# A recurrence with decay and a squared-ReLU network in one kernel: eight fewer matmuls on zeros ahead of the first dense layer, and new engine orders up to unit 4

## The chip, the core and the metric

The kernel runs on one core of a Trainium2 chip. Its engines work side by side: TensorE (PE) multiplies matrices, with weight loads (PEld) that overlap its matmuls; VectorE (DVE), ScalarE (ACT) and GpSimd (POOL) work element by element; SyncE (SP) and POOL issue transfers (DMA) between the chip's memory and the core's SBUF. PE writes into PSUM, in banks, from which DVE and ACT read.

The metric is the device time of one execution in microseconds (us). Each kernel is run several times, and the median counts. A profile is one further execution, recorded by the hardware profiler.

## The reference

```python
B, H, S, D = 4, 8, 768, 48
state = np.zeros((B, H, D, D)); y = np.zeros_like(q)
for t in range(S):
    state = alpha[:, :, t, :, None] * state + np.einsum('bhd,bhe->bhde', k[:, :, t], v[:, :, t])
    y[:, :, t] = np.einsum('bhd,bhde->bhe', q[:, :, t], state)
x = y.transpose(0, 2, 1, 3).reshape(B * S, H * D)     # 3072 x 384
r = np.maximum(x @ w_in, 0.0)                         # 384 -> 2048
out = (r * r) @ w_out                                 # 2048 -> 384
```

A linear attention with a decay `alpha` per channel, then two dense layers with a squared ReLU between them. `alpha` lies between 0.8 and 1.

## The kernel before

**Units.** Time is cut into three stretches of 256 steps. A *unit* is one stretch of one of the four sequences, so there are twelve, numbered 0 to 11 (units 0 to 3 are the first stretch of the four). Each unit passes through the same stages, and the work of several units overlaps.

**Names.** Every operation has a name, `kind` plus unit (and part), and these names make up the tables of the change. In a unit g:

- `lda ldk ldq ldv`: the four loads (384 KB each). Units 1 and 2 load from POOL's list, all others from SP's.
- `pr` (product of two neighbours' alpha), `ln` (its logarithm), `m1i`, `m1s` (matmuls that sum logarithms along time, into PSUM bank W), `ei ea ec es` (exponentials of the sums), `lm lb` (a difference that replaces `m1s` from unit 4 on), `bk aq` (one more factor alpha): the *decays*. Units 0 and 1 do without pairs: one matmul step `m1` (for unit 0 two, `m10`, `m11`, by halves of the heads).
- `ekm eqm`: keys and queries times their decays. `tr`: their transposes, on PE for units 0 to 2 (with copies `et` out of PSUM), from unit 3 on as two transposing DMAs `tr0 tr1` that SP issues. `vc`: v cast to bf16.
- `p0` (unit 0: also `p1`): the scores, keys against queries, into banks X and Z; `mk0 mk1`: causal mask on the two halves, out of PSUM.
- `kv`: the new state's matmuls (into Z from unit 1 on; from unit 3 on they are part of the `y` of the unit before); `sa sc sd`: sums and decay of the state.
- `y`: the attention's output into X; `xe`: out of PSUM; `xt`, `xv`: its transpose (units 0 to 3 on PE with a copy `xv`, then by DMA).
- `s1_g_u`, u = 0 to 7: the first dense layer, six matmuls of 256 columns into one of two banks H in turn; `re`: ReLU out of the bank; `sq`: the square, mostly of two groups at once.
- `s2_g_j_s`: the second layer, four matmuls of 384 columns; four groups make one output half j in the single bank O; `oe`: out of PSUM; `out`: the store.
- `win0 win1 wout0 wout1`: halves of the two weights, loaded and cast to bf16 from POOL's list. `s2` groups 0 and 1 read the first half of `wout`, 2 and 3 the second.
- `~512`, `~256` on PE: a matmul of that many columns on zeros into bank O. It waits for nothing but the zeros themselves, and nothing reads what it writes.

**What sets the order.** `TABLES` (L203 to L262) holds one list per engine, written out by name. `Program.schedule` takes each engine's queue from it word by word; an operation that several engines can do (`pr`, `sd`, `re`, `sq`, `oe`, `xv`, `et`, `vc`, `bk`) runs on the engine whose list names it. Dependencies come from the tiles that an operation reads and writes; `place` turns them into waits on semaphores ahead of the operation. An engine works through its list in order, so an operation that waits holds up all that stand behind it. That holds for SP and POOL too: a transfer is issued when all ahead of it in the list have been issued or done.

The fillers are placed here:

```python
if word[0] == "~":
    after, n = filler[0], int(word[1:])
    o = Op({"pe": (filler[1](n), 0)}, 0, "fill")
```

Some loads are gated by the landing of another:

```python
AFTER = {1: (0, "a"), ("win", 0): (0, "k"), ("win", 1): (0, "k"), 2: ("win", 0), ("wout", 0): ("win", 1),
         ("wout", 1): (2, "k"), 3: ("wout", 0)}
```

So `wout1` waits for unit 2's keys, and unit 3's loads for `wout0`. A bank is reused only after what was in it has been read: `s1_g_u` waits for the `re` of the group two before it in its bank, `s2_g_j_0` for the `oe` of the half before it, `m1s` for the exponentials that read `m1i`'s sums.

Of the kernel before, what the change touches and what calls it, by code (L numbers as in the profile page):

```python
# [24 lines left out]
class Program:  # L25
# [144 lines left out]
    def emit(self):  # L170
# [44 lines left out]
        s1_5_7 s1_5_6 s2_5_0_0 s2_5_0_1 s2_5_0_2 s1_6_0 s1_6_1 p0_7 s1_6_2 s1_6_3 s2_5_0_3 s1_6_4 s1_6_5 y7 m1i9
        s2_5_1_0 s2_5_1_1 s2_5_1_2 s2_5_1_3 s1_6_6 p0_8 s1_6_7 s2_6_0_0 s2_6_0_1 s1_7_0 s2_6_0_2 s1_7_1 s2_6_0_3
        s1_7_2 s1_7_3 y8 s1_7_5 s1_7_4 s2_6_1_0 s2_6_1_1 m1i10 s2_6_1_2 s1_7_7 s1_7_6 s2_6_1_3 s1_8_1 s1_8_0
        s2_7_0_0 s2_7_0_1 s2_7_0_2 s2_7_0_3 m1i11 s1_8_3 s1_8_2 p0_9 s2_7_1_0 s2_7_1_1 s1_8_4 s2_7_1_2 y9 s1_8_5
        s2_7_1_3 s1_8_6 s1_8_7 s2_8_0_0 s2_8_0_1 p0_10 s2_8_0_2 s1_9_1 s1_9_0 s2_8_0_3 s1_9_3 s1_9_2 y10 s1_9_5
# [872 lines left out]
```

## Time and profile before

| | us |
|---|---|
| median of 3 runs | 177.73 (177.08 to 179.05) |
| the profiled execution | 174.4 |
| its span, first to last instruction | 172.7 |
| first matmul of the first dense layer | 17.59 |
| last piece of the chain of waits | 170.39 |

Start times in the views below count from the span's start. The profiled execution is 1.7 us longer than its span, and 3.3 us shorter than the median of the runs. The granted TensorE clock in the page is 9 tenths or more in every slice. The share of the sixteen DMA engines in use is nine tenths or more in nearly every slice up to 100 us. In a row of the timeline the columns are start, length, engine, line, operation, output and inputs with their shapes, the number of instructions merged, and in brackets the idle time of the engine before it with what ended it. Line numbers are those of the kernel: `s1` is L965, `s2` L1005, ReLU L973 (ACT) and L975 (DVE), squares L983 and L987, scores L838, masks L849, fillers L1061, `pr` L565 and L567, `sd` L815, loads L456, weights L432, transposing DMAs L652.

### The profile page before, as it was taken

Reading aid. Unit: us, or ns where it says so; the run is one execution under the profiler, and the core shown is the slowest. Engines: PE = TensorE matmul, PEld = TensorE weight load, DVE = VectorE, ACT = ScalarE, POOL = GpSimd, SP = SyncE. Lnnn points to the kernel's source line nnn. Section 1 sums busy time; section 2 is a strip of 40 time slices with the busy share of each in tenths; the row PEclk is TensorE's granted clock in tenths of the full one; section 3 lists DMA queues with packets and bytes.
Section 4 is the critical chain, followed back from the end, with each engine's and each line's share of the span. In section 5 each row is a group of like instructions: output and inputs, shape, how many; then the busy total and the mean of one; then the engine's idle time right before and its main releaser. Section 6 shows DMA issues by size and latency. Waiting matters only on the chain.

```text
span 172.7 us, 5090 instructions
## 1 busy us (share of the span) xinstructions
PE 167.6 (97%) x2232; PEld 130.4 (76%) x2234; DVE 122.3 (71%) x202; ACT 113.7 (66%) x201; POOL 26.9 (16%) x37
## 2 busy tenths in 40 slices
...
GB/s 145 351 292 212 270 233 172 283 286 297 204 213 191 232 257 168 273 243 188 255 165 128 285 149 245 270 90 286 277 66 238 174 77 181 4 53 87 0 93 91
DMA packets 71030, 33.36 MB, mean 193 GB/s; under 512 B 67552, under 2 KB 67808, under 8 KB 71008
## 3 DMA queue, kind: packets, MB, share of 16 engines
...
## 4 chain that ended last, share of the span: by engine, by line
PE 79%; DMA 16%; POOL 3%; issue 1%; DVE 0%
PE psO L1005 34%; PE psWH L965 33%; DMA wout<-in_moe_w_out_dram 5%; DMA win<-in_moe_w_in_dram 5%; DMA raw<-in_k_dram 3%; POOL raw L456 3%; PE psX L735 2%; PE psZ L703 2%; DMA raw<-in_alpha_dram 2%; PE psX L838 2%; PE psX L724 2%; PE psX L935 2%; PE psZ L838 1%; PE psWH L574 1%; PE psX L909 0%
## 5 line engine op out<-in xcount | busy, mean ns | idle before, releaser
L965 PE MATMUL psWH<-xt,win 128*128 128x256 bf16 x576 | 73.0, 274 | 0.0
L1005 PE MATMUL psO<-wout,gt 128*128 128x384 bf16 x368 | 68.2, 326 | 0.6 <-DMA wout<-in_moe_w_out_dram 0.6
L965 PEld LDWEIGHTS psWH<-xt,win 128*128 128x128 bf16 x576 | 65.2, 145 | 4.6 <-ACT xt L923 0.4
L973 ACT ACTIVATE rr<-psWH 128x512 bf16<-128x512 f32 x70 | 41.3, 595 | 21.9 <-PE psWH L965 20.8
L1005 PEld LDWEIGHTS psO<-wout,gt 128*128 128x128 bf16 x368 | 35.0, 98 | 19.0 <-DMA wout<-in_moe_w_out_dram 0.8
L987 ACT ACTIVATE gt<-rr 128x1024 bf16<-128x1024 bf16 (+1 forms) x31 | 26.9, 890 | 3.5 <-DVE rr L975 3.1
L975 DVE TENSOR_SCALAR rr<-psWH 128x512 bf16<-128x512 f32 x26 | 17.7, 688 | 10.0 <-PE psWH L965 9.7
L983 DVE TENSOR_TENSOR gt<-rr 128x1024 bf16<-128x1024 bf16 (+1 forms) x29 | 17.2, 597 | 9.6 <-ACT rr L973 9.4
L631 POOL CAST vbf<-raw 128x768 bf16<-128x768 f32 x9 | 8.1, 899 | 68.3 <-DMA raw<-in_v_dram 68.3
L849 DVE TENSOR_TENSOR pm<-psX,caus 128x1024 bf16<-128x1024 f32 x12 | 14.6, 1220 | 4.0 <-PE psZ L838 4.0
L849 DVE TENSOR_TENSOR pm<-psZ,caus 128x1024 bf16<-128x1024 f32 x12 | 14.6, 1219 | 3.4 <-PE psZ L838 3.4
L1012 ACT ACTIVATE osb<-psO 128x384 f32<-128x384 f32 x14 | 6.9, 491 | 10.1 <-PE psO L1005 8.8
L1061 PE MATMUL psO<-zero 128*128 128x512 bf16 (+1 forms) x32 | 9.9, 437 | 1.5 <-DVE zero L376 1.3
L894 ACT ACTIVATE xbf<-psX 128x768 bf16<-128x768 f32 x10 | 8.1, 808 | 4.5 <-PE psX L724 4.1
L636 DVE TENSOR_TENSOR qks<-raw,eq 128x384 bf16<-128x384 f32 x18 | 10.5, 587 | 0.4 <-ACT eq L611 0.3
L641 DVE TENSOR_TENSOR qks<-raw,ek 128x768 bf16<-128x768 f32 x11 | 10.5, 954 | 0.1
L585 ACT ACTIVATE ek<-psWH 128x384 f32<-128x384 f32 x10 | 4.9, 489 | 5.9 <-PE psWH L574 3.8
L567 POOL TENSOR_TENSOR prd<-raw 128x384 f32<-128x384 f32 x6 | 6.2, 1035 | 16.3 <-DMA raw<-in_alpha_dram 16.3
L1014 DVE COPY osb<-psO 128x384 f32<-128x384 f32 x9 | 5.0, 555 | 4.8 <-PE psO L1005 4.6
L594 DVE TENSOR_TENSOR ek<-ek,raw 128x384 f32<-128x384 f32 x9 | 5.0, 553 | 3.7 <-ACT ek L585 3.7
L568 ACT ACTIVATE lab<-prd 128x384 bf16<-128x384 f32 x10 | 5.2, 518 | 2.4 <-POOL prd L567 1.4
L1061 PEld LDWEIGHTS psO<-zero 128*128 128x128 bf16 x34 | 3.2, 109 | 4.5 <-issue 1.9
...
## 6 DMA issues: line engine op xcount, KB each, us to landing
...
```

Of the source, the lines that this page charges most:

```text
L631: add("pool", lambda e: e.tensor_copy(vout, vin), 830, p0 + 900, reads=[("raw", r, 3)], writes=[("vbf", vb)], name=f"vc{g}", alts={"act": ...
L636: add("dve", lambda e, j=j, dst=dst: e.tensor_tensor(dst, RAW[r][:, 2, :, j, :].rearrange("p (n x) d -> p n x d", x=2), EQ[la][:, j].rearr ...
L641: add("dve", lambda e, a=a, E=E: e.tensor_tensor(QKS[qs][:, a, :, :, 0:D], RAW[r][:, 1 + a].rearrange("p h j d -> p j h d"), E[la][:].rear ...
L849: add("dve", lambda e, hf=hf, psT=psT: e.tensor_tensor(PM[pm][:, hf].rearrange("p r n j t -> p (r n) (j t)"), psT[:, :, :].rearrange("p r ...
L894: add("act", lambda e: e.activation(XBF[x2][:], psX[:, :, 0:HD], AF.Copy), act_ns(2 * HD), p0 + 6100, reads=[("ps", "X", 0), ("ps", "X", 1 ...
L965: ins = pe.matmul(psH[hb][:, i * T:(i + 1) * T], WIN[:, kk, hidden(fj)], mov, start=(kk == 0), stop=(kk == KT - 1))
L973: add("act", lambda e, hb=hb, rr=rr: e.activation(rr, psH[hb], AF.Relu), act_ns(512), pu + 600, reads=[("ps", "H", hb)], writes=[("rr", rb ...
L975: alts={"dve": (lambda e, hb=hb, rr=rr: e.tensor_scalar(rr, psH[hb], 0.0, None, ALU.max), dve_ns(512))})
L983: add("dve", lambda e, dst=dst, sq=sq: e.tensor_tensor(dst, sq, sq, ALU.mult), 148 + k * 267, pu + 1200, reads=[("rr", rb, h) for h in ran ...
L987: "act": (lambda e, dst=dst, sq=sq: e.activation(dst, sq, AF.Square), act_ns(k * 512))})
L1005: ins = pe.matmul(psS, GT[gt][:, fj, j, :], WOUT[:, fj, :], start=(fj == 0), stop=(fj == FT - 1))
L1061: pr.schedule(TABLES, (zero, lambda n: lambda pe: pe.matmul(psO[:, 0:n], ZERO[:, 0:128], ZERO[:, 0:n], skip_group_check=True)))
```

## The change

Only the five lists of `TABLES` are changed; no operation and no dependency is, apart from the fillers.

- On PE, the fillers ahead of unit 0's first layer go from thirty of 512 and four of 256 columns to twenty-six of 512.
- On PE, up to unit 4, `m1`, `s1` and `s2` groups change places: `m1i2` stands behind `s1_0_6` and `xt1`, `m1s2` behind `s1_1_0`; `s1_1_4` stands where `s1_1_5` stood, and `s1_1_5` and `s1_1_6` now stand ahead of `s2_0_0_2`; `p0_3` and `p0_4` stand one group earlier.
- Between engines: `pr2` from POOL to DVE, `sd1` from DVE to POOL ahead of `wout1` and `ldv2`; `pr4` and `pr6` from DVE to POOL, `pr7` from POOL to DVE; `vc6` from POOL to ACT; `re`, `sq`, `oe` and `xv` of units 0 to 4 are dealt anew between ACT and DVE (among them `sq0_1`, `re0_6` and `oe1_0` to DVE; `re0_4`, `sq0_3`, `oe0_1` and `xv3` to ACT).
- On DVE, `eqm0_4` stands behind `mk1_3`, `mk0_3`, `re2_5` and `sq2_1`.
- On SP, `lda5` stands ahead of `ldq4` and `ldk4`, `ldv4` behind unit 3's two transposes, `ldk5` and `out0_1` ahead of `lda6`.

Lines of a list that only break elsewhere are left out:

```diff
--- before
+++ after
 TABLES = {
     "pe": """
-        ~512 ~512 ~512 ~512 ~512 ~512 ~512 ~512 ~512 m10_0 m11_0 ~512 ~512 ~512 tr00_0 ~512 ~512 ~512 tr10_0 ~512
-        ~512 ~512 ~512 tr11_0 p0_0 ~256 ~256 kv0 tr01_0 ~512 ~512 ~512 ~512 ~512 p1_0 m11 ~256 y0 ~512 ~512 ~512
-        ~512 ~512 tr0_1 xt0 tr1_1 ~512 ~256 s1_0_0 s1_0_1 p0_1 s1_0_2 s1_0_3 kv1 s1_0_4 s1_0_5 y1 m1i2 s1_0_6 xt1
-        s1_0_7 m1s2 s1_1_0 s1_1_1 tr0_2 s1_1_2 s1_1_3 tr1_2 s2_0_0_0 s1_1_5 s2_0_0_1 p0_2 s2_0_0_2 s2_0_0_3 s1_1_7
-        s1_1_4 kv2 s2_0_1_0 m1i3 s2_0_1_1 s2_0_1_2 s2_0_1_3 s1_1_6 m1s3 y2 s2_1_0_0 m1i4 s2_1_0_1 xt2 s2_1_0_2
-        s2_1_0_3 s1_2_1 s1_2_0 s2_1_1_0 s1_2_3 s1_2_2 m1i5 s2_1_1_1 s1_2_4 p0_3 s1_2_5 s1_2_6 s2_1_1_2 s2_1_1_3 y3
-        s1_2_7 s2_2_0_0 xt3 m1i6 s2_2_0_1 s1_3_1 s1_3_0 s2_2_0_2 s1_3_3 s1_3_2 s2_2_0_3 p0_4 s1_3_5 s1_3_4 s2_2_1_0
-        s2_2_1_1 s2_2_1_2 s2_2_1_3 y4 s1_3_7 s1_3_6 s2_3_0_0 s2_3_0_1 p0_5 m1i7 s2_3_0_2 s2_3_0_3 s1_4_1 s1_4_0 y5
-        s1_4_3 s1_4_2 s2_3_1_0 s2_3_1_1 s1_4_4 s1_4_5 s2_3_1_2 s2_3_1_3 s1_4_6 s1_4_7 s2_4_0_0 s1_5_0 s1_5_1
...
+        ~512 ~512 ~512 ~512 ~512 ~512 ~512 ~512 ~512 m10_0 m11_0 ~512 ~512 tr00_0 ~512 ~512 tr10_0 ~512 ~512 ~512
+        tr11_0 p0_0 ~512 kv0 tr01_0 ~512 ~512 ~512 ~512 p1_0 m11 y0 ~512 ~512 ~512 ~512 tr0_1 xt0 tr1_1 ~512 s1_0_0
+        s1_0_1 p0_1 s1_0_2 s1_0_3 kv1 s1_0_4 s1_0_5 y1 s1_0_6 xt1 m1i2 s1_0_7 s1_1_0 m1s2 s1_1_1 tr0_2 s1_1_2 s1_1_3
+        tr1_2 s2_0_0_0 s1_1_4 s2_0_0_1 p0_2 s1_1_5 s1_1_6 s2_0_0_2 s2_0_0_3 s1_1_7 kv2 s2_0_1_0 m1i3 s2_0_1_1
+        s2_0_1_2 m1s3 s2_0_1_3 y2 s2_1_0_0 m1i4 s2_1_0_1 xt2 s2_1_0_2 s2_1_0_3 s1_2_1 s1_2_0 s2_1_1_0 s2_1_1_1
+        s1_2_2 s1_2_3 m1i5 p0_3 s2_1_1_2 s1_2_5 s1_2_4 s2_1_1_3 y3 s1_2_7 s1_2_6 xt3 s2_2_0_0 s2_2_0_1 s1_3_1
+        s2_2_0_2 s2_2_0_3 s1_3_0 m1i6 s1_3_3 p0_4 s1_3_2 s2_2_1_0 s1_3_5 s2_2_1_1 s2_2_1_2 s1_3_4 y4 s2_2_1_3 s1_3_6
+        s1_3_7 s2_3_0_0 s2_3_0_1 p0_5 m1i7 s2_3_0_2 s2_3_0_3 s1_4_1 s1_4_0 y5 s1_4_2 s1_4_3 s2_3_1_0 s2_3_1_1 s1_4_4
+        s1_4_5 s2_3_1_2 s2_3_1_3 s1_4_6 s1_4_7 s2_4_0_0 s1_5_0 s1_5_1 s2_4_0_1 s2_4_0_2 m1i8 s1_5_2 s2_4_0_3 p0_6
...
     """,
     "act": """
         table copycaus ln0_0 ln1_0 ei0_0 ea0_0 ei1_0 ea1_0 ec0_0 ec1_0 et00_0 et10_0 vc0 ln1 vc1 ei1 ea1 xe0 ec1 xv0
-        re0_0 re0_1 sq0_1 re0_2 re0_3 ln2 xe1 ei2 ea2 re0_6 ec2 re0_7 es2 re1_0 re1_1 sq0_5 re1_3 et1_2 sq1_1 sq1_3
-        oe0_0 ln3 ei3 ea3 re1_7 ec3 sq1_5 ln4 es3 re1_6 xe2 ei4 ea4 lm4 oe1_0 re2_1 ec4 re2_0 ln5 es4 re2_2 ei5
-        re2_3 re2_4 lm5 ea5 ec5 re2_5 sq2_1 sq2_5 oe1_1 xe3 ln6 re2_6 sq2_7 sq2_6 es5 re3_1 re3_0 ei6 ea6 re3_3 ec6
-        re3_2 oe2_0 re3_5 ln7 lm6 re3_4 sq3_5 xe4 re3_6 sq3_7 ei7 es6 ea7 oe3_0 re4_1 xe5 ec7 lm7 re4_2 sq4_3 re4_4
-        re4_5 sq4_5 oe3_1 re4_7 ln8 es7 ei8 re5_2 oe4_0 lm8 re5_3 ea8 re5_4 re5_5 xe6 oe4_1 es8 re5_7 sq5_7 sq5_6
...
+        re0_0 re0_1 re0_2 re0_3 sq0_3 re0_4 xe1 ln2 ei2 ea2 ec2 re0_7 es2 re1_1 sq0_7 re1_2 et1_2 re1_5 sq1_5 re1_6
+        oe0_0 ln3 re1_7 ei3 ea3 ec3 es3 oe0_1 ln4 xe2 ei4 ea4 lm4 ec4 re2_0 ln5 re2_1 re2_2 ei5 ea5 es4 sq2_3 re2_4
+        xe3 re2_7 ec5 lm5 xv3 re2_6 sq2_6 ln6 es5 re3_0 re3_3 lm6 re3_2 ei6 ea6 ec6 re3_5 re3_4 oe2_1 es6 xe4 ln7
+        re3_7 sq3_7 sq3_6 ei7 vc6 re4_1 re4_0 xe5 sq4_3 ea7 re4_4 re4_5 sq4_5 ec7 oe3_1 re4_7 lm7 ln8 es7 ei8 re5_2
+        oe4_0 lm8 re5_3 ea8 re5_4 re5_5 xe6 oe4_1 es8 re5_7 sq5_7 sq5_6 re6_0 re6_1 re6_2 re6_3 re6_4 ln9 re6_5 xe7
...
     """,
     "dve": """
         zzero zlinc zlstr zident zcaus zcaus1 zones zown zlaf0 own0 zlaf1 own1 zqks0 zqks1 zqks2 zlab0 zlab1 ekm0_0
-        eqm0_0 eqm1_0 ekm1_0 et11_0 mk0_0 et01_0 sa0 mk1_0 sc0 sd0 ekm1 eqm1 et0_1 et1_1 mk1_1 mk0_1 sa1 re0_4 re0_5
-        sq0_3 sc1 sd1 xv1 bk2 ekm2 aq2 sq0_7 eqm2 re1_2 sq0_6 et0_2 re1_5 mk1_2 mk0_2 pr3 sa2 re1_4 sc2 bk3 ekm3 pr4
-        oe0_1 sd2 sq1_7 aq3 sq1_6 eqm0_3 sa3 eqm1_3 xv2 bk4 eqm1_4 ekm4 pr5 lb4 sc3 eqm0_4 sd3 mk0_3 mk1_3 lb5 sq2_3
-        pr6 re2_7 xv3 eqm1_5 ekm5 sa4 sc4 sd4 bk6 eqm0_5 sq3_3 mk0_4 mk1_4 lb6 oe2_1 sq3_1 sa5 sc5 re3_7 ekm6 sq3_6
-        mk1_5 mk0_5 bk7 sd5 re4_0 sa6 re4_3 sq4_1 lb7 eqm1_6 sc6 eqm0_6 ekm7 eqm1_7 re4_6 sq4_6 sq4_7 re5_0 re5_1
...
+        eqm0_0 eqm1_0 ekm1_0 et11_0 mk0_0 et01_0 sa0 mk1_0 sc0 sd0 ekm1 eqm1 et0_1 et1_1 mk1_1 mk0_1 sa1 sq0_1 sc1
+        pr2 re0_5 xv1 re0_6 bk2 ekm2 re1_0 aq2 eqm2 et0_2 sq1_1 re1_3 sq0_5 sq0_6 re1_4 mk0_2 mk1_2 pr3 sq1_3 sa2
+        sc2 bk3 ekm3 aq3 sq1_6 sa3 eqm0_3 eqm1_3 sq1_7 sd2 xv2 sc3 bk4 oe1_0 pr5 lb4 ekm4 sd3 eqm1_4 re2_3 mk1_3
+        mk0_3 re2_5 sq2_1 eqm0_4 oe1_1 sq2_5 lb5 sq2_7 sa4 re3_1 sc4 ekm5 sd4 oe2_0 eqm1_5 eqm0_5 mk1_4 mk0_4 sq3_1
+        bk6 lb6 pr7 sq3_3 sq3_5 sa5 sc5 re3_6 ekm6 mk1_5 mk0_5 bk7 oe3_0 re4_2 re4_3 ekm7 eqm1_6 sq4_1 eqm1_7 eqm0_6
+        sd5 sa6 re4_6 sc6 sq4_6 lb7 sq4_7 re5_0 re5_1 eqm0_7 sq5_1 bk8 mk0_6 mk1_6 eqm1_8 ekm8 lb8 sq5_3 sq5_5 re5_6
...
     """,
     "pool": """
-        slinc slstr sident scaus scaus1 lda1 ldk1 ldq1 ldv1 win0 win1 lda2 ldk2 ldq2 wout0 pr2 wout1 ldv2 vc2 vc3
-        vc4 bk5 pr7 vc5 vc6 vc7 pr8 vc8 pr9 vc9 pr10 pr11 vc11
+        slinc slstr sident scaus scaus1 lda1 ldk1 ldq1 ldv1 win0 win1 lda2 ldk2 ldq2 wout0 sd1 wout1 ldv2 vc2 vc3
+        pr4 vc4 bk5 pr6 vc5 vc7 pr8 vc8 pr9 vc9 pr10 pr11 vc11
     """,
     "sp": """
-        lda0 ldk0 ldq0 ldv0 lda3 ldv3 ldk3 lda4 ldq3 ldq4 ldk4 lda5 ldv4 tr1_3 tr0_3 lda6 ldq5 tr1_4 ldk5 tr0_4
-        out0_1 lda7 ldv5 ldk6 tr1_5 tr0_5 ldv6 xt4 out1_1 ldq6 ldk7 ldq7 ldv7 xt5 lda8 tr1_6 tr0_6 out2_1 ldk8 ldq8
+        lda0 ldk0 ldq0 ldv0 lda3 ldv3 ldk3 lda4 ldq3 lda5 ldq4 ldk4 tr1_3 tr0_3 ldv4 ldk5 out0_1 lda6 ldq5 tr1_4
+        tr0_4 ldv5 lda7 ldk6 tr1_5 tr0_5 ldv6 xt4 out1_1 ldk7 ldq6 ldq7 xt5 ldv7 lda8 tr1_6 tr0_6 out2_1 ldk8 ldq8
         tr1_7 tr0_7 xt6 ldv8 lda9 out3_1 tr1_8 tr0_8 ldq9 xt7 ldv9 ldk9 lda10 out4_1 lda11 tr1_9 xt8 ldk10 ldq10
         out5_1 tr0_9 ldv10 ldv11 tr0_10 tr1_10 xt9 ldk11 ldq11 out6_1 out7_1 xt10 tr0_11 tr1_11 out8_1 xt11 out9_1
```

More of the change, by code (lines that the diff above doesn't have):

```diff
@@ L215 @@
[L215 to L219, printed above, removed]
@@ new lines @@
+        s2_2_0_2 s2_2_0_3 s1_3_0 m1i6 s1_3_3 p0_4 s1_3_2 s2_2_1_0 s1_3_5 s2_2_1_1 s2_2_1_2 s1_3_4 y4 s2_2_1_3 s1_3_6
+        s1_3_7 s2_3_0_0 s2_3_0_1 p0_5 m1i7 s2_3_0_2 s2_3_0_3 s1_4_1 s1_4_0 y5 s1_4_2 s1_4_3 s2_3_1_0 s2_3_1_1 s1_4_4
+        s1_4_5 s2_3_1_2 s2_3_1_3 s1_4_6 s1_4_7 s2_4_0_0 s1_5_0 s1_5_1 s2_4_0_1 s2_4_0_2 m1i8 s1_5_2 s2_4_0_3 p0_6
+        s1_5_3 s1_5_4 s2_4_1_0 s2_4_1_1 s1_5_5 y6 s2_4_1_2 s2_4_1_3 s1_5_7 s1_5_6 s2_5_0_0 s2_5_0_1 s2_5_0_2 s1_6_0
+        s1_6_1 p0_7 s1_6_2 s1_6_3 s2_5_0_3 s1_6_4 s1_6_5 y7 m1i9 s2_5_1_0 s2_5_1_1 s2_5_1_2 s2_5_1_3 s1_6_6 p0_8
```

31 lines of the change are left out of this document (16 added, 15 removed).

## The prediction

> **What bounds the kernel now.** I read the page's first part, then the chain of waits, then the timeline engine by engine up to 62 us, where most of what is reordered lies: PE's list is the old one again from `s2_3_1_0` on.
>
> ```profile
> PE 167.6 (97%) x2232; PEld 130.4 (76%) x2234; DVE 122.3 (71%) x202; ACT 113.7 (66%) x201; POOL 26.9 (16%) x37
> ```
>
> TensorE (PE) is busy nearly all the time. The chain of waits says from where on it sets the end, here around 33 us in order of time (start, length, what) and as its shares on the page:
>
> ```profile
> 33.17 0.05 issue
> 33.22 1.47 PE psO L1005 x8
> 34.69 1.31 PE psWH L965 x12
> ```
> ```profile
> PE 79%; DMA 16%; POOL 3%; issue 1%; DVE 0%
> ```
>
> 33.2 of 172.7 us is 19%, and that is all of the chain's DMA and POOL: behind 33.22 it holds PE work and almost nothing else. So a change ahead of 33 us is worth what PE has done *more* by then, and a change behind it can only cost, by idling PE. PE waits for the second half of `wout` until just before 33.22 (its row stands below). The unit of account comes from here: twelve `s1` matmuls are two groups, 1.31 us, so a group is 0.655.
>
> **The matmuls on zeros.** Row by row before the first dense layer (timeline, start and length):
>
> ```profile
> 11.09 1.03 PE L1061 MATMUL psO<-zero 128*128 128x512 bf16 x4
> 12.05 0.42 PE L838 MATMUL psZ<-kqt 64*64 64x128 bf16 x16
> ```
> ```profile
> 11.13 0.41 DVE L529 COPY kqt<-psZ 128x512 bf16<-128x512 bf16 x1
> ```
> ```profile
> 12.56 0.84 ACT L632 ACTIVATE vbf<-raw 128x768 bf16<-128x768 f32 x1 [1.95 <-DMA raw<-in_v_dram]
> ```
>
> `p1_0` (12.05) needs the copy that ended at 11.54, and starts only when the zeros in front are through: here they are on the path. Of the five there four show; they fill 11.09 to 12.05, at most 0.24 each, 0.2 with something for the change of shape. One of the five goes, so `p1_0` and what follows on DVE (`mk1_0`, `sc0`, `sd0`, `ekm1`) move up by 0.2, and `tr0_1`, `xt0`, `xv0` and `s1_0_0` with them. Everywhere else PE waits for ACT or DVE with or without zeros. Bounds: 0, because `ei1` follows `vc1` (13.40), which waited for a load; and eight times 0.24 = 1.9, if all eight delayed something. I take 0.2, by the one place where the releaser had ended half a microsecond earlier.
>
> **Unit 2's decays, the core of the change.** `pr2` leaves POOL for DVE, `sd1` goes the other way, and `m1i2` moves behind `s1_0_6` and `xt1`. Before:
>
> ```profile
> 23.79 0.34 PE L574 MATMUL psWH<-lab,linc 128*128 128x384 bf16 x1
> 23.97 0.24 PE L577 MATMUL psWH<-ones,lab 128*128 128x2 bf16 x4
> 24.07 0.86 PE L965 MATMUL psWH<-xt,win 128*128 128x256 bf16 x6
> 24.77 0.51 PE L909 MATMUL psX<-ident,xbf 128*128 128x128 bf16 x6
> 25.11 0.83 PE L965 MATMUL psWH<-xt,win 128*128 128x256 bf16 x6
> 26.23 0.34 PE L574 MATMUL psWH<-lab,lstr 128*128 128x384 bf16 x1 [0.29 <-ACT acm L590]
> 26.40 0.82 PE L965 MATMUL psWH<-xt,win 128*128 128x256 bf16 x6
> ```
> ```profile
> 22.01 0.55 DVE L804 TENSOR_TENSOR smd<-psZ,own 128x384 bf16<-128x384 f32 x1
> 22.48 1.31 DVE L975 TENSOR_SCALAR rr<-psWH 128x512 bf16<-128x512 f32 x2
> 23.71 0.68 DVE L983 TENSOR_TENSOR gt<-rr 128x1024 bf16<-128x1024 bf16 x1
> 24.30 0.55 DVE L811 TENSOR_TENSOR tmp<-psZ,smd 128x384 f32<-128x384 f32 x1
> 24.89 0.56 DVE L815 TENSOR_TENSOR sbd<-tmp,acm 128x384 bf16<-128x384 f32 x1
> 25.37 0.55 DVE L921 COPY xt<-psX 128x768 bf16<-128x768 bf16 x1
> 25.84 0.55 DVE L594 TENSOR_TENSOR ek<-ek,raw 128x384 f32<-128x384 f32 x1
> 26.42 0.96 DVE L641 TENSOR_TENSOR qks<-raw,ek 128x768 bf16<-128x768 f32 x1
> ```
> ```profile
> 22.92 0.53 ACT L568 ACTIVATE lab<-prd 128x384 bf16<-128x384 f32 x1 [1.10 <-POOL prd L567]
> 23.90 0.81 ACT L894 ACTIVATE xbf<-psX 128x768 bf16<-128x768 f32 x1 [0.46 <-PE psX L771]
> ```
> ```profile
> 21.87 1.01 POOL L567 TENSOR_TENSOR prd<-raw 128x384 f32<-128x384 f32 x1 [0.36 <-DMA raw<-in_alpha_dram]
> 24.01 0.60 POOL L432 DMA_DIRECT2D wout<-in_moe_w_out_dram  x1 [1.13 <-DMA raw<-in_k_dram]
> 24.61 0.91 POOL L456 DMA_DIRECT2D raw<-in_v_dram  x1
> 34.53 0.83 POOL L631 CAST vbf<-raw 128x768 bf16<-128x768 f32 x1 [9.01 <-DMA raw<-in_v_dram]
> ```
>
> I step through the new lists by these durations (on DVE an independent successor starts some 0.08 before its forerunner's end, as 25.84 does, a dependent one just after it). The 0.2 gained puts the end of `sa1` (the `smd` row) at 22.35. DVE then does `sq0_1` (0.68), `sc1` (0.55) and `pr2` (0.55, the price of `sc1`, same shape), ending at about 23.9; ACT is in `xe1` (the `xbf` row, 0.2 earlier) until 24.5 and in `ln2` (the `lab` row) until 24.95. PE meanwhile: `s1_0_6` in `m1i2`'s place at 23.6, idle 0.2, `xt1` at 24.56, done at 25.07, `m1i2` at 25.0, `s1_0_7` at 25.24 until 25.9. `s1_1_0` now needs `xv1` and, behind it, `re0_6` (half of the 1.31 row), both on DVE: 25.10 + 0.55 + 0.65, so 26.31 with what a release takes, an idle 0.4. Before, that group began at 26.40 with `m1s2` (0.16) done. So the lead is nearly gone here: the 0.3 that PE waited for `acm` at 26.23 goes, and `re0_6` is what comes last next.
>
> DVE goes on without a pause: `bk2`, `ekm2` (to 27.7), `re1_0` (28.3), `aq2`, `eqm2` (29.8). So `tr1_2` runs at 29.84, and `s2_0_0_0`, `s1_1_4` and `s2_0_0_1` behind it put `p0_2` at 32.33; PE stands still 0.15 for each of `re1_0` and `eqm2`. Before:
>
> ```profile
> 31.97 0.42 PE L838 MATMUL psX<-kqt 64*64 64x128 bf16 x16
> 32.22 0.39 PE L838 MATMUL psZ<-kqt 64*64 64x128 bf16 x16
> 33.22 0.99 PE L1005 MATMUL psO<-wout,gt 128*128 128x384 bf16 x5 [0.60 <-DMA wout<-in_moe_w_out_dram]
> ```
>
> So `p0_2` is 0.36 later. Behind `p0_2` two more groups (`s1_1_4` instead of `s1_1_5` had stood ahead of it; `s1_1_5` and `s1_1_6` now follow) run before the second half of `wout` is used, at about 34.36. Before, it was used at 33.22; with the 1.31 us of extra work that equals 34.53. Gain so far 0.17: the 0.60 us wait for `wout` is gone, but almost all of it is paid in the small waits just named.
>
> **What POOL now delays.** `sd1` stands ahead of `wout`'s second half and of `ldv2`. It needs `sc1` (23.42) and costs about 1.0 by the `prd` row, also an elementwise product of 384 columns; so those two are issued at 24.5 to 24.8, 0.5 to 0.8 late. Landing moves by 0 (if the other transfers end earlier instead) to 0.8: `wout` at 33.2 to 34.0, hidden until 34.36; `vc2` ends at 35.4 to 36.2, hidden until `kv2` at 36.4 (34.36, two `s2` groups of 0.65 and one `s1` group, and the change of tile shape). I take nothing for either; without that cover the second costs at most what `vc2` overruns, 0.3 if it is 0.5 worse.
>
> **Units 3 and 4.** SP now issues `ldv4` behind unit 3's two transposes, and `eqm0_4` comes late on DVE (behind `mk0_3`, `re2_5`, `sq2_1`):
>
> ```profile
> 40.46 1.16 SPq L456 DMA_DIRECT2D raw<-in_v_dram  x1
> 43.54 3.17 SPq L652 DMA_TRANSPOSE kqt<-qks  x2
> ```
> ```profile
> 46.50 0.83 POOL L631 CAST vbf<-raw 128x768 bf16<-128x768 f32 x1 [9.03 <-DMA raw<-in_v_dram]
> ```
> ```profile
> 52.78 0.09 PEld L724 LDWEIGHTS psX<-smd,kqt 64*128 64x128 bf16 x1 [0.32 <-DVE pm L849]
> ```
> ```profile
> DMA to landing us min/median/max: 3.6/4.1/5.9
> ```
> ```profile
> 60.37 0.26 PEld L838 LDWEIGHTS psX<-kqt 64*64 64x64 bf16 x16 [0.32 <-DVE qks L636]
> ```
>
> `ldv4` before: issued 40.46, used at 46.50, 6.0 us later. Now the transposes start at about 42.8 (DVE has `pr4`, `oe0_1` and `sd2` no longer ahead of them, but waits for `kv3` then) and SP is free at 46.0; `vc4` would end between 51 and 52.9 (landing after 4.2 to 6.0), and `y3`, which wants it, comes at 52.1 (52.78 less one group, which now stands behind it). The fifth row is the landing of the transposes. `eqm0_4` ends at 53.5 (`mk0_3` 0.3 ahead of `y3` as before, then 0.65, 0.68 and 0.55 less the overlaps); two issues of 1.6, and 4.1 more give 59.2 for `tr0_4` (61.0 at worst), against `p0_4` at 59.8 (60.37 less the group that moved behind it). Both just hold. For `oe1_0` on DVE and `re2_1` behind `ln5` I find PE waiting 0.1 each, so +0.2.
>
> **Sum.** -0.2 (zeros) + 0.03 (the stretch to 34.36) + 0.2 (units 2 to 4) = about 0 on the profiled 174.4 us (span 172.7). Places with a margin under 0.7 us (`kv2`, `y3`, `p0_4`) can only add; I put 0.1 there. The runs shown have their median at 177.73, 3.3 above the profiled execution, and I carry the difference over: 177.8. A measurement of this kernel can tell about 1%, 1.8 us, from no change.
>
> **The clock.** Nine zeros at the start took long:
>
> ```profile
> 1.25 4.02 PE L1061 MATMUL psO<-zero 128*128 128x512 bf16 x9 [1.25 <-DVE zero L376]
> ```
>
> That is 0.45 each, against 0.24 or less later. The Trainium skill (TensorE: Matmul & The Clock Gate, "What's actually happening") has the clock halved after an idle window of some 3.4 us; the trace agrees that PE starts slow and is fast after 4 us, and by this rule the change costs nothing, since the gaps that open stay near half a microsecond. The same page ("PE-mode transpose") says that transposes do not count as busy in the same way, which speaks against thinning the zeros around them; no row here shows the clock falling again.
>
> **Rivals.** *Forecast*, chance 0.45: what is gained is given back, 177.5 (without the last two terms) to 178.4 (the three narrow places 0.2 each).
>
> *The waits on DVE don't come*, 0.22: the steps 26.31, 28.4 and 29.84 are worked out by durations and could each be earlier. Then 0.2, the 0.3 at `m1s2` and the 0.6 at `wout` all stay: 1.1 less, 176.6. For: the same two waits are in the rows. Against: DVE has no pause from 25.1 on in the new list.
>
> *The transposes of unit 4 take the place of `wout`*, 0.25, the case that ends slower: `tr0_4` lands after `p0_4` is next on PE. It decides once `eqm0_4` ends later than about 54, or SP is still held at that time; price the landing's spread, 61.0 less 59.8, and the overrun of `vc4` at `y3` (0.8) if that comes too: 0.8 to 2.0, 178.5 to 179.7. For: both stand on SP behind other issues. Against: a later `y3` moves `p0_4` too, so they overlap.
>
> *The clock falls back*, 0.03: half speed over one stretch like the first, 4.02 less 9 x 0.24, 1.9 us: 179.7.
>
> *The zeros were all spare*, 0.05: PE waits instead, the 0.2 is not there: 178.0.
>
> Range 176.4 to 179.6: the lower end takes in the full gain with a little for `wout`, the upper the landing's spread. Faster by over 1% needs more than every wait named: 0.06. Slower by over 1% is the upper part of the transposes' case and the clock: 0.16. Within 1%: 0.78.
>
> **What would show it.** `s1_0_0` 0.2 earlier; PE idle before `s1_1_0` with DVE's `re0_6` (L975) as releaser; no PE wait for `wout`, first use near 34.4; `wout` issued at 24.5 or later behind `sbd` on POOL; `p0_4` not released by a transpose. PE waiting for `kqt` from DMA near 60 us, or for `vbf` near 36 or 52, would prove the slower case; `s1_1_0` before 26 the faster one.

## The result, and the profile after

| | before | changed |
|---|---|---|
| median of 22 runs each, us | 175.87 (174.68 to 179.05) | 177.03 (175.24 to 180.37) |
| ratio to before, 95% interval | 1 | 1.0061 [1.0035, 1.0086] |
| profiled execution (span), us | 174.4 (172.7) | 178.41 (176.7) |

The changed kernel is slower by 0.6%, 1.1 us. The ratio leaves out the longest executions, which count as a slower state, and the profiled execution of the changed kernel is one of these. The forecast of 177.8 us stood on the older median of before, 177.73; against a before of 175.87 its "no change" would have been 175.9. The absolute time came out closer than the reasoning deserves, and that is luck: the level of the runs fell by 1.9 us, and the change cost 1.1 us where the sum had about 0.

In the profiled execution unit 1's `v` landed late (`vc1` starts at 13.93 instead of 12.56, behind a wait for its load), which moves the first dense layer from 17.59 to 18.48. So its times are read against each other here, and the mechanism from the experiments. First the page's busy times, and its shares of the chain of waits:

```profile
PE 167.3 (95%) x2224; PEld 129.4 (73%) x2226; DVE 127.1 (72%) x208; ACT 109.9 (62%) x195; POOL 26.3 (15%) x37
...
PE 58%; DMA 18%; DVE 8%; SPq 6%; ACT 4%; issue 2%; POOL 2%; ACTq 0%
```

PE's work is the same (167.6 before), and its share of the chain falls from 79% to 58%. Before, nothing but PE's work stood in the chain behind 33.22, up to 0.28 us of DVE at the very end; now DVE, SP's queue and transfers hold pieces far behind it. Some pieces of that chain, in order of time (start, length, what):

```profile
47.13 1.31 SPq L651
48.49 5.07 DMA raw<-in_v_dram
...
83.03 1.90 SPq L651
84.98 4.68 DMA out_dram<-osb
...
120.84 6.08 DMA kqt<-qks
```

The first four are twice the same picture: SP is held by a pair of transposing DMAs (L651), and what stands behind them in its list is issued late: first unit 4's `v`, then a store. The last piece is a transpose of unit 9. The timeline of PE has the places where this reaches it, with the wait in brackets:

```profile
27.42 0.87 PE L964 MATMUL psWH<-xt,win 128*128 128x256 bf16 x6 [0.21 <-DVE rr L974]
51.01 0.42 PE L837 MATMUL psX<-kqt 64*64 64x128 bf16 x16 [0.78 <-DMA kqt<-qks]
54.58 0.18 PE L723 MATMUL psX<-smd,kqt 64*128 64x48 bf16 x1 [0.21 <-POOL vbf L630]
62.60 0.42 PE L837 MATMUL psX<-kqt 64*64 64x128 bf16 x16 [0.32 <-DVE osb L1013]
90.29 1.47 PE L1004 MATMUL psO<-wout,gt 128*128 128x384 bf16 x8 [0.31 <-ACT osb L1011]
```

The first is the forecast wait before `s1_1_0`, and the wait for `wout` at 33.22 is gone, as forecast. The other four are new: `p0_3` waits for unit 3's transposes, `y3` for `vc4`, `p0_4` for what the next paragraph names, and a second-layer group for an output buffer that a store still reads. A fifth, 0.40 at `p0_9` (126.97), ends with the transpose of the chain above; in before `p0_9` did not wait.

The bracket of `p0_4` names DVE's copy, but that copy had ended a quarter of a microsecond earlier:

```profile
61.80 0.55 DVE L1013 COPY osb<-psO 128x384 f32<-128x384 f32 x1
```

Unit 4's second transposing DMA was issued at 57.72 and landed 4.8 later, at 62.51, which is 0.09 ahead of `p0_4`. In e4_oldsp below, where no releaser is named at `p0_4`, the landing (62.17) is again 0.09 ahead of it (62.26). So, as far as these times can tell, the transposes ended this wait.

POOL has what was moved to it:

```profile
24.61 1.07 POOL L812 TENSOR_TENSOR sbd<-tmp,acm 128x384 bf16<-128x384 f32 x1 [2.34 <-DVE tmp L810]
25.63 0.60 POOL L431 DMA_DIRECT2D wout<-in_moe_w_out_dram  x1
...
53.61 0.82 POOL L630 CAST vbf<-raw 128x768 bf16<-128x768 f32 x1 [11.29 <-DMA raw<-in_v_dram]
```

`sd1` costs 1.07 there (1.0 was taken), and `wout1` is issued 1.6 later than the 24.01 of before, of which 0.9 is this execution's late start.

### The profile page after: what moved, and what is told of

Same layout as the page of the kernel before. It is cut to its first block, busy times and chain, and to the rows that moved or that the text cites. A ratio compares the mean times of both kernels' runs of the same rounds, so it can differ in the third digit from the quotient of the medians.

```text
span 176.7 us, 5076 instructions
## 1 busy us (share of the span) xinstructions
PE 167.3 (95%) x2224; PEld 129.4 (73%) x2226; DVE 127.1 (72%) x208; ACT 109.9 (62%) x195; POOL 26.3 (15%) x37
## 4 chain that ended last, share of the span: by engine, by line
PE 58%; DMA 18%; DVE 8%; SPq 6%; ACT 4%; issue 2%; POOL 2%; ACTq 0%
PE psWH L964 24%; PE psO L1004 22%; DMA raw<-in_v_dram 7%; DMA out_dram<-osb 6%; DMA kqt<-qks 3%; SPq L651 2%; SPq L455 2%; DMA raw<-in_alpha_dram 2%; PE psZ L702 2%; PE psX L734 2%; PE psX L837 2%; POOL raw L455 2%; PE psX L934 2%; PE psX L723 1%; DVE rr L974 1%
## 5 line engine op out<-in xcount | busy, mean ns | idle before, releaser
L972 ACT ACTIVATE rr<-psWH 128x512 bf16<-128x512 f32 x68 | 40.2, 595 | 28.3 <-PE psWH L964 27.3
L982 DVE TENSOR_TENSOR gt<-rr 128x1024 bf16<-128x1024 bf16 (+1 forms) x33 | 20.9, 640 | 9.3 <-ACT rr L972 9.1
L986 ACT ACTIVATE gt<-rr 128x1024 bf16<-128x1024 bf16 (+1 forms) x27 | 22.5, 849 | 4.9 <-DVE rr L974 4.5
L974 DVE TENSOR_SCALAR rr<-psWH 128x512 bf16<-128x512 f32 x28 | 19.0, 686 | 8.9 <-PE psWH L964 8.6
L630 POOL CAST vbf<-raw 128x768 bf16<-128x768 f32 x8 | 6.6, 824 | 80.6 <-DMA raw<-in_v_dram 80.6
L1011 ACT ACTIVATE osb<-psO 128x384 f32<-128x384 f32 x12 | 5.9, 491 | 9.5 <-PE psO L1004 7.6
L635 DVE TENSOR_TENSOR qks<-raw,eq 128x384 bf16<-128x384 f32 x18 | 9.6, 549 | 1.1 <-DMA raw<-in_q_dram 1.1
L1060 PE MATMUL psO<-zero 128*128 128x512 bf16 x24 | 8.0, 465 | 1.4 <-DVE zero L375 1.3
L1013 DVE COPY osb<-psO 128x384 f32<-128x384 f32 x11 | 6.1, 553 | 4.2 <-PE psO L1004 3.2
L837 PE MATMUL psX<-kqt 64*64 64x128 bf16 x192 | 5.0, 222 | 1.7 <-DMA kqt<-qks 1.2
```

The lines of the kernel that those rows point to most:

```text
L635: add("dve", lambda e, j=j, dst=dst: e.tensor_tensor(dst, RAW[r][:, 2, :, j, :].rearrange("p (n x) d -> p n x d", x=2), EQ[la][:, j].rearr ...
L837: ins = pe.matmul(psT[64 * c:64 * c + 64, rr_, o:o + 128], keys, mov)
L972: add("act", lambda e, hb=hb, rr=rr: e.activation(rr, psH[hb], AF.Relu), act_ns(512), pu + 600, reads=[("ps", "H", hb)], writes=[("rr", rb ...
L974: alts={"dve": (lambda e, hb=hb, rr=rr: e.tensor_scalar(rr, psH[hb], 0.0, None, ALU.max), dve_ns(512))})
L982: add("dve", lambda e, dst=dst, sq=sq: e.tensor_tensor(dst, sq, sq, ALU.mult), 148 + k * 267, pu + 1200, reads=[("rr", rb, h) for h in ran ...
L986: "act": (lambda e, dst=dst, sq=sq: e.activation(dst, sq, AF.Square), act_ns(k * 512))})
```

## The experiments

All times are medians of 12 runs (e4_oldsp and e12_unit3: 6) beside the kernel before on the same chip; only the ratios compare across groups, since the median of before lay between 176.0 and 176.9 in them.

### The parts alone

**e1_zeros**: before, with the new zeros only.

```diff
-        m11_0 ~512 ~512 ~512 tr00_0 ~512 ~512 ~512 tr10_0 ~512 ~512 ~512 ~512 tr11_0 p0_0 ~256 ~256 kv0 tr01_0
-        ~512 ~512 ~512 ~512 ~512 p1_0 m11 ~256 y0 ~512 ~512 ~512 ~512 ~512 tr0_1 xt0 tr1_1 ~512 ~256 s1_0_0
+        m11_0 ~512 ~512 tr00_0 ~512 ~512 tr10_0 ~512 ~512 ~512 tr11_0 p0_0 ~512 kv0 tr01_0
+        ~512 ~512 ~512 ~512 p1_0 m11 y0 ~512 ~512 ~512 ~512 tr0_1 xt0 tr1_1 ~512 s1_0_0
```

> The kernel before with nothing changed but the matmuls on zeros: thirty of 512 and four of 256 columns become twenty-six of 512. The late theory (the loss lies behind unit 2's output, in the new order of units 3 and 4 and on SP) expects 0.2 us faster than before, ratio 0.999, with p1_0 earlier by 0.2 and the granted work of PE otherwise the same. The early theory (the loss lies in unit 2's later decays) expects the same 0.999. A third theory, that the zeros kept something going (PE's speed or the front's pace), expects the whole loss here: 1.004 to 1.008.

Measured: 175.94 us, 0.9987 [0.9952, 1.0023]. PE's rows:

```profile
17.30 1.53 PE L965 MATMUL psWH<-xt,win 128*128 128x256 bf16 x12 [0.24 <-ACT xt L923]
25.95 0.34 PE L574 MATMUL psWH<-lab,lstr 128*128 128x384 bf16 x1 [0.19 <-ACT acm L590]
33.37 1.48 PE L1005 MATMUL psO<-wout,gt 128*128 128x384 bf16 x8 [1.03 <-DMA wout<-in_moe_w_out_dram]
```

The first layer starts 0.29 earlier, the wait for `wout` grows from 0.60 to 1.03. Alone, the gain is given back at `wout`, whose second half was used no earlier in this execution (33.37) than in before (33.22).

**e2_early**: the new zeros and the new lists of PE, ACT, DVE and POOL up to unit 2's output `y2`; behind it the lists of before, and SP's list of before. **e3_late**: the opposite cut, with SP's new list. The joint in DVE's list (`xv2` is where the stretch behind `y2` begins):

```diff
 e2_early against before
-        bk3 ekm3 pr4 oe0_1 sd2 sq1_7 aq3 sq1_6 eqm0_3 sa3 eqm1_3
+        bk3 ekm3 aq3 sq1_6 sa3 eqm0_3 eqm1_3 sq1_7 sd2
         xv2 bk4 eqm1_4 ekm4 pr5 lb4 sc3 eqm0_4 sd3 mk0_3
 e3_late against before
         bk3 ekm3 pr4 oe0_1 sd2 sq1_7 aq3 sq1_6 eqm0_3 sa3 eqm1_3
-        xv2 bk4 eqm1_4 ekm4 pr5 lb4 sc3 eqm0_4 sd3 mk0_3
+        xv2 sc3 bk4 oe1_0 pr5 lb4 ekm4 sd3 eqm1_4 re2_3 mk1_3 mk0_3 re2_5 sq2_1 eqm0_4
```

> The new zeros and the new lists of PE, ACT, DVE and POOL up to unit 2's output y2; from there on the lists of before, and SP's list of before throughout. The early theory expects all of the loss: 1.004 to 1.008, with PE idle before s1_1_0 and y2 later than in the kernel before by 0.5 us or more. The late theory expects 0.997 to 1.001: the front's 0.2 us kept, y2 within 0.2 us of before, no wait for vbf near y3.

Measured: 175.93 us, 0.9988 [0.9950, 1.0026]. PE's rows:

```profile
26.49 0.88 PE L965 MATMUL psWH<-xt,win 128*128 128x256 bf16 x6 [0.22 <-DVE rr L975]
...
32.52 0.42 PE L838 MATMUL psX<-kqt 64*64 64x128 bf16 x16
...
34.46 1.46 PE L1005 MATMUL psO<-wout,gt 128*128 128x384 bf16 x8
```

> The zeros and the lists of before up to y2; from there on the new lists, and SP's new list throughout. The late theory expects the loss here: 1.004 to 1.010, with y3 waiting for unit 4's cast v (vbf from POOL after a late load) by 0.3 us or more and p0_3 or p0_4 waiting for a transpose. The early theory expects 0.999 to 1.002 and no such waits.

Measured: 177.18 us, 1.0051 [1.0011, 1.0091]. In order PE, SP and POOL:

```profile
49.47 0.42 PE L837 MATMUL psX<-kqt 64*64 64x128 bf16 x16 [0.38 <-DMA kqt<-qks]
53.98 0.18 PE L723 MATMUL psX<-smd,kqt 64*128 64x48 bf16 x1 [1.16 <-POOL vbf L630]
```
```profile
43.78 3.18 SPq L651 DMA_TRANSPOSE kqt<-qks  x2
47.01 1.27 SPq L455 DMA_DIRECT2D raw<-in_v_dram  x1
```
```profile
53.01 0.83 POOL L630 CAST vbf<-raw 128x768 bf16<-128x768 f32 x1 [15.28 <-DMA raw<-in_v_dram]
```

The part up to `y2` can't be told apart from no change, and the part behind it is where the loss lies. Here `ldv4`, issued when the transposes let SP go, landed 6.0 us later, and `y3` waited 1.16 for the cast.

### Is it one cause, the place of `ldv4`?

**e5_ldv4**: the changed kernel with `ldv4` back ahead of the transposes. **e6_before_ldv4late**: before, with `ldv4` behind them.

```diff
 e5_ldv4 against changed
-        lda0 ldk0 ldq0 ldv0 lda3 ldv3 ldk3 lda4 ldq3 lda5 ldq4 ldk4 tr1_3 tr0_3 ldv4 ldk5
+        lda0 ldk0 ldq0 ldv0 lda3 ldv3 ldk3 lda4 ldq3 lda5 ldq4 ldk4 ldv4 tr1_3 tr0_3 ldk5
 e6_before_ldv4late against before
-        ldq4 ldk4 lda5 ldv4 tr1_3 tr0_3 lda6
+        ldq4 ldk4 lda5 tr1_3 tr0_3 ldv4 lda6
```

> The changed kernel with one word moved on SP: ldv4 ahead of unit 3's two transposes, where it stood in the kernel before. SP stands idle there, so nothing else need be later. If ldv4's place is the cause: y3 does not wait for vbf, and the time is 0.996 to 1.000 of the kernel before (1.0 to 1.4 us below the changed kernel). If the cause is elsewhere in the late part (DVE's order, the transposes' landing): 1.003 to 1.007, with PE waiting for a transpose at p0_3 or p0_4 in place of vbf.

Measured: 177.35 us, 1.0061 [1.0020, 1.0103]. The wait at `y3` is gone, and PE waits in three places:

```profile
49.88 0.42 PE L837 MATMUL psX<-kqt 64*64 64x128 bf16 x16 [0.68 <-DMA kqt<-qks]
70.20 0.42 PE L837 MATMUL psX<-kqt 64*64 64x128 bf16 x16 [0.26 <-DMA kqt<-qks]
88.79 1.47 PE L1004 MATMUL psO<-wout,gt 128*128 128x384 bf16 x8 [0.47 <-ACT osb L1011]
```

> The kernel before with one word moved on SP: ldv4 behind unit 3's two transposes. If ldv4's place alone makes the loss, it appears here: 1.004 to 1.010, with y3 at 53.9 us or later waiting for vbf (the load issued near 46.8, landing 6 us later, the cast 0.8). If the new lists of DVE and PE are needed for it: 0.998 to 1.002.

Measured: 176.56 us, 1.0018 [0.9974, 1.0062], which can be told apart neither from no change nor from the 1.0051 of e3_late. The wait that was expected at `y3` did not come: `vc4` ended at 53.30 and `y3` started at 53.54. But `p0_4` waited 0.74 for DVE, which had itself waited 2.44 for unit 5's keys, a load further back on SP, and `p0_5` waited 0.49. The theory of a single cause falls with the first of the two: with the wait at `y3` taken away nothing was gained. The waits at `p0_3` and for the store had stood beside it in the changed kernel already.

### SP's order

**e4_oldsp**: the changed kernel with SP's list of before (around units 3 and 4).

```diff
-        lda5 ldq4 ldk4 tr1_3 tr0_3 ldv4 ldk5 out0_1 lda6 ldq5 tr1_4 tr0_4 ldv5 lda7 ldk6
+        ldq4 ldk4 lda5 ldv4 tr1_3 tr0_3 lda6 ldq5 tr1_4 ldk5 tr0_4 out0_1 lda7 ldv5 ldk6
```

> The changed kernel with SP's list of before, so that ldv4 is issued ahead of unit 3's two transposes again and out0_1 behind unit 4's. If the late theory holds because of SP's order, the loss is mostly gone: 0.998 to 1.003, no wait for vbf at y3. If it holds because of DVE's order (eqm0_4 late) or the early theory holds, it stays at 1.004 to 1.008.

Measured: 180.46 us, 1.0230 [1.0167, 1.0292]. SP's rows behind 50 us:

```profile
55.25 1.26 SPq L651 DMA_TRANSPOSE kqt<-qks  x1
56.56 1.08 SPq L455 DMA_DIRECT2D raw<-in_k_dram  x1
57.69 1.92 SPq L651 DMA_TRANSPOSE kqt<-qks  x1
59.65 1.43 SPq L1022 DMA_DIRECT2D out_dram<-osb  x1
```

`tr1_4` waits for DVE's late products, and `ldk5`, `tr0_4` and the store `out0_1` are held behind it; PE then waits 1.45 at `p0_3`, 0.78 at `p0_4`, 0.70 for DVE's copy into an output buffer, and 0.91 for ACT's near 91. So SP's new order goes with DVE's late `eqm0_4`: with SP's old order the same lists of the other engines lose more.

### Giving DVE its margin back

Both start from e5_ldv4: **e7_ldv4_re06** moves `re0_6` ahead of `xv1`, **e8_ldv4_eqm04** moves `eqm0_4` directly behind `mk0_3`.

```diff
 e7_ldv4_re06
-        pr2 re0_5 xv1 re0_6 bk2 ekm2
+        pr2 re0_5 re0_6 xv1 bk2 ekm2
 e8_ldv4_eqm04
-        mk0_3 re2_5 sq2_1 eqm0_4 oe1_1
+        mk0_3 eqm0_4 re2_5 sq2_1 oe1_1
```

> As the run with ldv4 ahead of the transposes, and on DVE re0_6 ahead of xv1 instead of behind it: DVE stands idle 0.6 us there until unit 1's transpose is through, and re0_6 is ready. If the step by step reading of the early part holds, s1_1_0 starts 0.4 us earlier (26.0 to 26.1 instead of 26.5) and about 0.3 of it stays until y2: 0.994 to 0.999 of the kernel before. If the later waits on DVE (eqm2, re1_0) hold the early part anyway, it equals the run without the move.

Measured: 177.19 us, 1.0064 [1.0023, 1.0105], not the 0.994 to 0.999 that was expected if the gain stayed. In its profile `y2` starts at 40.28 instead of 40.60, as expected, but the next place takes it:

```profile
49.67 0.42 PE L837 MATMUL psX<-kqt 64*64 64x128 bf16 x16 [0.79 <-DMA kqt<-qks]
```

> As the run with ldv4 ahead of the transposes, and on DVE eqm0_4 directly behind mk0_3 instead of behind re2_5 and sq2_1 as well, so unit 4's transposes start 1.2 us earlier. If p0_4 becomes the next wait once y3 is early (a transpose landing after PE is ready), this run is 0.3 to 0.8 us faster than the run without the move: 0.992 to 0.998. If p0_4 does not wait, the two agree, or s1_2_7 waits for re2_5 and it is up to 0.4 us slower.

Measured: 177.26 us, 1.0072 [1.0030, 1.0114]. No gain. In its profile unit 4's transposes start at 53.95 (54.62 in e5_ldv4) and `p0_4` does not wait, but it did not in e5_ldv4 either; `p0_3` waits 1.22 and `p0_6` 1.07, both for transposes.

### `p0_3` and its transposes

Both start from e5_ldv4. **e9_p03** puts one group back ahead of `p0_3`; **e10_tr3** moves the products that the transposes need ahead of `sa3`, which waits for `kv3`.

```diff
 e9_p03
-        m1i5 p0_3 s2_1_1_2 s1_2_5 s1_2_4 s2_1_1_3 y3
+        m1i5 s1_2_4 p0_3 s2_1_1_2 s1_2_5 s2_1_1_3 y3
 e10_tr3
-        aq3 sq1_6 sa3 eqm0_3 eqm1_3 sq1_7
+        aq3 sq1_6 eqm0_3 eqm1_3 sa3 sq1_7
```

> The kernel of e5_ldv4 (changed kernel, ldv4 ahead of unit 3's transposes) with one PE group put back: s1_2_4 stands ahead of p0_3 again instead of behind s1_2_5. Theory (several landings without margin behind y2, each swallowing about half a microsecond): p0_3 comes one group (0.65) later, so its wait for kqt from DMA (0.68 there) goes and y3 is 0.2 to 0.6 earlier than 53.18; the waits at p0_5 and at the store near 88 stay: ratio 1.002 to 1.005 of the kernel before. Rival (the lists lose by PE's order itself, or by the engines' loads, not by landings): 1.005 to 1.008, unchanged, with the wait gone but PE idle elsewhere.

Measured: 177.93 us, 1.0055 [1.0017, 1.0094].

```profile
52.71 0.19 PE L723 MATMUL psX<-smd,kqt 64*128 64x48 bf16 x1 [0.40 <-DVE pm L848]
...
88.22 1.47 PE L1004 MATMUL psO<-wout,gt 128*128 128x384 bf16 x8 [0.46 <-ACT osb L1011]
```

The wait at `p0_3` is gone. But only three groups now lie between `p0_3` and `y3` where before had four, so that `y3` waits 0.40 for the mask; `p0_5` waits 0.18, and the store near 88 still costs 0.46. The ratio lies just outside the 1.002 to 1.005 that was expected, and can't be told from that of e5_ldv4.

> The kernel of e5_ldv4 with eqm0_3 and eqm1_3 ahead of sa3 on DVE, so that they do not wait for kv3. Theory: unit 3's transposes start 0.5 to 1.0 earlier than 43.41, p0_3 loses its wait for kqt (0.68 there); sa3, sd2 come up to 1.0 later, hidden behind PE's groups; y3 0.3 to 0.6 earlier; ratio 1.002 to 1.005. Rival (SP or the transfers are what holds them): start unchanged at 43.4, ratio 1.006.

Measured: 177.31 us, 1.0038 [1.0003, 1.0073], within what was expected; but in the profile the transposes do not start earlier. SP:

```profile
42.72 2.89 SPq L455 DMA_DIRECT2D raw<-in_v_dram  x1
45.65 4.12 SPq L651 DMA_TRANSPOSE kqt<-qks  x2
```

The issue of `ldv4` held SP until 45.6, though the products had ended at 43.5. In that execution, one of the two longest of its twelve, SP was the bound, as the rival had it, and `p0_3` waited 2.44. The ratio and the one profile point different ways: inconclusive.

### A kernel meant to be faster, and a finer cut

**e11_best**: e2_early with both moves on DVE (`re0_6` ahead of `xv1`, `eqm0_3 eqm1_3` ahead of `sa3`). **e12_unit3**: e5_ldv4 with the lists of before for PE, ACT, DVE and POOL behind unit 3 (`pr6` stays on POOL). The joint on PE:

```diff
 e12_unit3 against e5_ldv4
         y3 s1_2_7 s1_2_6 xt3 s2_2_0_0
-        s2_2_0_1 s1_3_1 s2_2_0_2 s2_2_0_3 s1_3_0 m1i6 s1_3_3 p0_4 s1_3_2
+        m1i6 s2_2_0_1 s1_3_1 s1_3_0 s2_2_0_2 s1_3_3 s1_3_2 s2_2_0_3 p0_4
```

> The kernel of e2_early (changed kernel up to y2, kernel before behind it and on SP) with re0_6 ahead of xv1 and eqm0_3, eqm1_3 ahead of sa3 on DVE. Theory: the first move brings y2 0.3 earlier than 40.25; the second makes the transposes of unit 3 start about 1 us earlier than 43.39, so that p0_3 (49.99 there) can use the 0.3; behind it the old lists hold their margins: 0.992 to 0.997 of the kernel before. Rival (the next landing takes it, at p0_4 or p0_5): 0.997 to 1.001.

Measured: 175.94 us, 0.9966 [0.9929, 1.0003]: the lowest ratio of all, and not yet told apart from no change. In its profiled execution transfers were late (PE waits 0.46 for `win`, 0.16 for `wout`, 0.67 before `p0_3`), so `y2` came at 41.02 and the expected 0.3 can't be seen.

> The kernel of e5_ldv4 up to unit 3 (PE up to xt3 and s2_2_0_0, the other lists up to the same set of operations), with the lists of PE, ACT, DVE and POOL of the kernel before behind that; SP as in e5_ldv4. If the loss lies in units 3's lists (p0_3's wait): 1.004 to 1.007, no gain against e5_ldv4. If it lies behind them (p0_5, the store near 88): 1.000 to 1.003, with p0_3 still waiting 0.5 to 0.8 and no wait at p0_5. If each is worth about half: 1.002 to 1.004.

Measured: 178.86 us, 1.0137 [1.0099, 1.0175], outside all that was expected. In order SP, POOL and PE:

```profile
49.93 2.06 SPq L455 DMA_DIRECT2D raw<-in_alpha_dram  x1
```
```profile
55.99 1.11 POOL L566 TENSOR_TENSOR prd<-raw 128x384 f32<-128x384 f32 x1 [5.23 <-DMA raw<-in_alpha_dram]
```
```profile
59.05 0.34 PE L573 MATMUL psWH<-lab,linc 128*128 128x384 bf16 x1 [1.81 <-ACT lab L567]
```

SP's new list issues `lda6` behind `ldk5` and `out0_1`; POOL's `pr6` waits for it, ACT's `ln6` for that, and PE's list of before has `m1i6` five groups earlier than the new one. The kernel doesn't divide the loss between units 3 and 4; it shows again that the lists fit only as a set.

## Why the prediction was right, and where not

**Zeros, -0.2.** `s1_0_0` came 0.29 earlier (e1_zeros), 0.2 (e5_ldv4) and 0.02 (e2_early, where PE waited for `win` instead). In time the term can't be seen: 0.9987 with 0.35% to either side.

**Unit 2's decays.** This walk held: `s1_1_0` forecast 26.31 with `re0_6` last, measured 26.49 in e2_early with DVE's ReLU as releaser; `p0_2` 32.33, measured 32.52; second half of `wout` 34.36 without a wait, measured 34.46 without one. In e5_ldv4, where the first layer did start 0.2 earlier, the three are 26.33, 32.36 and 34.30. The gain at `wout` was paid in small waits on DVE ahead of it, and the part up to `y2` as a whole came out at 0.9988. That POOL delays `wout1` cost nothing while PE came late enough; in e11_best, whose transfers were late, PE waits 0.16 for it.

**Units 3 and 4, +0.2, and narrow places, +0.1.** Here is the error: two terms, 0.3 together, that were sized too small. The whole change less its early part is 1.0061 - 0.9988 = 0.0073, or 1.3 us, with about 0.0046 to either side; the late part alone is 1.0051, or 0.9 us. I had 0.3. A table shows where, between points that have the same PE work ahead of them in both lists (differences of start times in the timeline, `y` taken at its first matmul on `vbf`; single executions scatter by some 0.5 us, as before and e2_early show, which have the same lists behind `y2`):

| us | `y2` to `p0_5` | `p0_5` to `y6` | `y6` to `y11` |
|---|---|---|---|
| before | 28.37 | 20.12 | 62.12 |
| e2_early | 28.81 | 20.11 | 62.33 |
| e3_late | 30.05 | 20.11 | 62.56 |
| changed | 30.15 | 20.60 | 62.58 |
| e5_ldv4 | 29.60 | 20.77 | 62.24 |
| e9_p03 | 29.31 | 20.74 | 62.49 |

Against e2_early, the changed kernel and e3_late lose 1.2 to 1.3 by `p0_5`, e5_ldv4 0.8; from there to `y6` all but e3_late lose another 0.5 to 0.7. PE does not work longer, it waits longer: the waits behind `y2` that are named above come to 2.0 us in the changed kernel's profile (with `p0_9`), and to none in before. Three steps of the prediction failed here.

First, `p0_3` was not among the narrow places. The change moves it one group (0.65) forward, and I priced only the same move of `p0_4`. The margin could have been read from the rows of before: two transposes issued from 43.54 on in 3.17, so the second at about 45.1, plus a median landing of 4.1, make 49.2, and `p0_3` started at 49.45. The trace has the landing itself, at 49.25: no wait stood there, and only 0.2 us of margin. Even the order of before waits here when its transposes land later: 0.20 in e1_zeros (landing at 49.78) and 0.24 in e2_early (49.90). e5_ldv4, with 0.68 at that place, paid the whole group back; e9_p03 took the wait away by undoing the move.

Second, unit 3's transposes were to start at 42.8 because three operations leave DVE ahead of them. They started at 43.41 in e5_ldv4 (44.50 in the changed kernel's long execution). One of the three, `pr4`, went to POOL, and there it took DVE's time after all (below). In e3_late, where all three are still ahead of them, they started at 43.78; with SP free at 47.0 instead of 46.0, `vc4` ended at 53.8, beyond the 51 to 52.9 that I gave, and `y3`'s margin was gone: 1.16. In the changed kernel SP was free at 48.5, of which 0.9 is the late start, and `y3` waited 0.21.

These two steps move `p0_4` as well. I had `eqm0_4` end 1.4 behind the start of `y3`, and so it did in e5_ldv4; but `y3` came at 53.2 instead of 52.1, `eqm0_4` ended at 54.6 instead of 53.5, and unit 4's transposes landed at 60.5 (61.5 in e3_late, 62.5 in the changed kernel) instead of 59.2. "Both just hold" was right for `p0_4` in e5_ldv4 and e3_late, and wrong by 0.32 in the changed kernel.

Third, I stopped where PE's list is the old one again, and so missed a change that goes on in DVE's list: `eqm0_6` now stands behind `ekm7` and `eqm1_7`. SP and ACT of e5_ldv4 have what follows:

```profile
79.96 3.16 SPq L651 DMA_TRANSPOSE kqt<-qks  x2
83.17 1.16 SPq L1022 DMA_DIRECT2D out_dram<-osb  x1
```
```profile
88.25 0.49 ACT L1011 ACTIVATE osb<-psO 128x384 f32<-128x384 f32 x1 [1.98 <-DMA out_dram<-osb]
```

Unit 6's transposes start when DVE ends `eqm0_6` (78.92 and 1.02 for two products, 79.94), the store behind them is issued at 83.17, and `oe` waits 1.98 for its buffer. In before the same `oe` waited 0.70 and PE did not notice; now PE's group at 88.79 waits 0.47. This chain is read from the profile; no run puts `eqm0_6` back. In e3_late, which has the same lists here, the store was issued at 83.75, `oe` got its buffer at 87.72, and PE did not wait: the place lies at the edge, as `p0_3` does.

**The rivals.** *The transposes of unit 4 take the place of `wout`* is the case that came nearest. Its condition, `eqm0_4` ending later than about 54, was met: 54.6 in e5_ldv4, 56.4 in the changed kernel (0.9 of it the late start). Its place, `p0_4`, waited 0.32 in the changed kernel, and its second leg, `vc4` at `y3`, 0.21 there and 1.16 in e3_late. It had no word for the other waits: `p0_3` (unit 3), in e5_ldv4 also `p0_5` (unit 5), the store behind unit 6's transposes and `p0_9`. The measured 1.1 lies within its price of 0.8 to 2.0, and its interval, 0.6 to 1.5, only touches the -0.2 to 0.7 of the case that I held likeliest, *what is gained is given back*. So the time lies in the range because the range is wide, not because the sum was right. *The waits on DVE don't come* is refuted by the releaser at 26.49; *the clock falls back* too: the longest gap, 1.54 in the changed kernel's long execution, left the eight matmuls behind it (16.52) at 0.62, as in before, and the recorded mean clock is 1.000.

**What stays open.** That the loss lies behind `y2` is shown by e2_early and e3_late. That no single wait carries all of it is shown by e5 and e9, which removed those at `y3` and at `p0_3` one after the other and stayed at 1.0061 and 1.0055; with 0.4% to either side they can't say what either is worth. How it divides among `p0_3`, `y3`, `p0_4`, `p0_5`, the store and `p0_9` is argued from single profiles; e12_unit3, meant to divide it, did not. No run takes all of them away with the new lists kept.
